# Sliding-window and linear attention in one kernel: value products as full matmuls, token sums in strips, a range check and a new order

## Chip, core and metric

One NeuronCore of one Trainium2 chip runs the whole program. The metric is device microseconds of one execution. Three runs of the kernel before gave 276.16, 276.88 and 277.05, median 276.88.

## What is computed

Two independent attention blocks, A and B, on inputs of 2048 tokens by 640 features (bf16), 32 heads of 20. A is softmax attention in which a token sees itself and the 255 before it; B is linear attention. Their outputs stand side by side in the result.

```python
# A
qkv = (x @ wqkv) split into q, k, v; heads of 20
scores = q k^T * 20**-0.5, kept where 0 <= i - j < 256
o = softmax(scores) v;  a = o @ wo
# B
phi(t) = where(t > 0, t + 1, exp(t)) + 1e-6
kv = phi(k)^T v;  z = sum over tokens of phi(k)
o = (phi(q) kv) / (phi(q) . z + 1e-6);  b = o @ wo
out = concatenate([a, b])
```

## The kernel before

**Order of the work.** Nothing is scheduled by a compiler. `build` describes some hundreds of operations to a `Planner` (line 56): each has the engines that may do it with an assumed duration, a key (its priority), the operations it depends on, and buffer slots. `Planner.run` (line 101) then plays the program through with these durations, takes the operation with the lowest key on each engine whenever the engine is free, and emits it at that point. So the instruction order of each engine is fixed when the program is built. On the chip every engine works its list in order and waits on semaphores. Nearly all DMAs are issued by one queue, SP, also in order; `dma` operations have keys and earliest times like the others.

**A.** Queries and keys of 512 tokens at a time (four tiles, t = 0 to 3) are projected by `proj` (line 374; matmuls at line 385) as 128x512 products. Heads are 20 wide and the tensor engine is addressed in strips of 32 rows, so 16 heads land in the tile `even` and the others are rearranged into `odd` by SBUF transfers on SP (lines 409 and 412). `proj_v` (line 426) makes the values: for each block of 64 tokens it issues two half-width matmuls per step (line 439), one for each half of the array's columns, so that a block's values of one set of heads come out on partitions 0 to 63 and those of the other set on 64 to 127. `attn` (line 463) then runs groups of heads: the score matmuls S (line 495) into the only big PSUM buffer, an exponential on ScalarE (line 507) with no maximum subtracted, masks on VectorE (line 517), and the product of probabilities and values, PV (line 538), with eight small tiles of the array side by side. Each value row carries a 21st column of ones, so PV gives the softmax sums too. The result goes to DRAM (`OD`, line 561) and comes back in another layout (`oc`, line 597; the sums alone as `osum`, line 601). Its reciprocal is taken by a logarithm and an exponential on ScalarE (lines 608 and 612), VectorE scales `oc` (line 621), and `finish_rows` (line 568, matmuls at line 573) multiplies by A's output matrix and stores.

**B.** `b_keys` (line 656) makes phi of the keys, `pk`. `b_sums` (line 673, matmuls at line 684) makes x^T phi(k); `b_z` (line 695) the token sums of phi(k), by 80 matmuls with one column of ones (line 714); `b_kvwo` (line 727) folds the value matrix and B's output matrix into one 640x640 matrix, which goes through DRAM for a new layout. `b_query` (line 802) makes phi of the queries (matmuls at line 811, evacuation at lines 636, 640 and 643), the denominator (`den`, line 823), its reciprocal (lines 827 and 834), scales (line 842) and ends in `finish_rows` again.

**The start.** Ten matmuls on a zeroed tile (line 855) run first. The first 512 tokens of x come as rows in four transfers (`x0n`, line 874) and are transposed on TensorE (line 902); all later ones come by transposing DMAs (`load_x`, line 353). The first halves of A's query and key weights (`wqn`, `wkn`) are issued by ScalarE's queue, the rest by SP (line 350), and are copied into the strip layout on VectorE (lines 891 and 895).

The values' half-width matmul, which a sentence hardly says:

```python
tok = bb * P + 64 * k0
rhs = wv[:, kt, :].rearrange("p (a i n) -> p a i n", a=2, i=2)[:, :, i, :]
nc.tensor.matmul(psum(g, k0, [P, 2, 160])[64 * i : 64 * i + 64, :, :], lhsT=xb["t"][:, kt, tok : tok + 64], rhs=rhs, ..., tile_position=(0, 64 * i))
```

## Time and profile before

| what | value |
|---|---|
| median of 3 runs | 276.88 us |
| the profiled execution's own time | not listed beside the profile |
| its span, first to last instruction | 273.2 us |
| TensorE busy | 255.1 us, 93% |
| ScalarE busy | 190.1 us, 70% |
| VectorE busy | 183.8 us, 67% |
| values, line 439 | 320 matmuls, 26.0 us busy |
| token sums, line 714 | 80 matmuls, 3.5 us busy |
| mean granted TensorE clock | 0.988 |

Busy times of matmuls are pipelined: the sum of the means is larger than the busy time, and the distance between starts in the timeline tells what one costs. PE is TensorE, PEld its weight loads, DVE VectorE, ACT ScalarE, POOL GpSimd; SPq is the instruction queue of the engine that issues the DMAs. In a row of groups the busy time is followed by the mean of one and by the idle time ahead of the group with what ended it. PEclk is the clock that TensorE was granted, in tenths of full speed.

### The profile page before, as it was taken

How to read it: one execution, taken by the hardware profiler on the slowest of the kernel's cores; microseconds unless marked ns; L12 is line 12 of the kernel's file. 1: busy time of each engine (PE TensorE's matmuls, PEld its weight loads, DVE VectorE, ACT ScalarE, POOL GpSimd, SP SyncE). 2: the span in 40 equal slices, each digit the busy share in tenths (PEclk: the TensorE clock that was granted, in tenths of full speed). 3: DMA queues.
4: the chain of work that ended last, by engine and by line, in shares of the span. 5: the costliest groups of instructions: out<-in, count | busy, mean ns of one | idle time of the engine just before them, and what ended most of it. 6: DMA issues, size and time to landing. Idle time of an engine off the chain costs nothing.

```text
span 273.2 us, 9860 instructions
## 1 busy us (share of the span) xinstructions
PE 255.1 (93%) x4312; PEld 148.0 (54%) x4312; DVE 183.8 (67%) x453; ACT 190.1 (70%) x187; POOL 6.8 (2%) x49
## 2 busy tenths in 40 slices
PE   7599998998998999989999999999989999999594
PEld 3245664545454556545556667457544665656273
DVE  1586776886776786678545444457896777788574
ACT  2066769779976888787868768378989869963410
POOL 8000000000000000001000000000000000000000
PEclk9999999999999999999999999599999999999999
DMA  7955535934448397556661104613999331302523
GB/s 204 313 106 68 171 91 119 148 95 67 104 121 148 85 261 225 120 153 96 191 198 37 44 0 129 154 49 91 203 193 231 90 113 56 108 24 89 163 81 111
DMA packets 51947, 34.50 MB, mean 126 GB/s; under 512 B 32066, under 2 KB 50754, under 8 KB 51906
## 3 DMA queue, kind: packets, MB, share of 16 engines
q1 hardware_dynamic: 50594, 33.08, 50.1%
q10 hardware_dynamic: 1312, 0.82, 1.1%
q8 instruction: 33, 0.54, 0.9%
q14 instruction: 8, 0.07, 0.1%
HBM read 13.80 MB, written 10.26 MB: 88 GB/s over the span
## 4 chain that ended last, share of the span: by engine, by line
PE 77%; DMA 7%; DVE 5%; SPq 4%; ACT 4%; issue 2%; ACTq 0%
PE F L573 16%; PE F L385 15%; PE F L684 9%; PE S L495 8%; PE F L439 8%; PE F L538 7%; PE F L661 6%; PE F L811 6%; SPq L361 3%; DMA wkn<-in_A_wqkv_dram 2%; ACT p L507 2%; DMA out_dram<-osb 2%; DMA osum<-OD 2%; PE F L823 1%; PE F L714 1%
## 5 line engine op out<-in xcount | busy, mean ns | idle before, releaser
L507 ACT ACTIVATE p<-S 128x2048 bf16<-128x2048 f32 x76 | 141.0, 1855 | 38.1 <-PE S L495 36.7
L517 DVE TENSOR_TENSOR p<-p,strip 128x256 bf16<-128x256 bf16 (+2 forms) x140 | 49.3, 381 | 21.0 <-ACT p L507 20.6
L636 ACT ACTIVATE e<-F 128x320 bf16<-128x320 f32 (+1 forms) x52 | 24.5, 500 | 9.1 <-PE F L811 7.7
L385 PE MATMUL F<-xT,wq 128*128 128x512 bf16 x100 | 25.3, 380 | 4.4 <-DMA xT<-in_A_x_dram 1.8
L385 PE MATMUL F<-xT,wk 128*128 128x512 bf16 x100 | 27.8, 406 | 0.0
L303 DVE CAST osb<-F 128x320 bf16<-128x320 f32 x45 | 21.9, 489 | 8.6 <-PE F L573 8.2
L303 DVE CAST even<-F 128x512 bf16<-128x512 f32 x29 | 20.0, 688 | 9.6 <-PE F L385 9.4
L439 PE MATMUL F<-wv,xT 128*64 128x320 bf16 x320 | 26.0, 302 | 0.4 <-issue 0.4
L661 PE MATMUL F<-wkB,xT 128*128 128x320 bf16 x160 | 25.6, 300 | 0.0
L573 PE MATMUL F<-kvwo,pq 128*128 128x320 bf16 x160 | 23.4, 299 | 2.0 <-DVE pq L842 2.0
L811 PE MATMUL F<-xT,wqB 128*128 128x512 bf16 x100 | 24.4, 381 | 0.9 <-DVE pq L643 0.9
L573 PE MATMUL F<-woA,oc 128*128 128x320 bf16 x160 | 24.7, 299 | 0.1
L684 PE MATMUL F<-pk,xtok 128*128 128x320 bf16 x160 | 24.5, 300 | 0.0
L538 PE MATMUL F<-p,v 64*32 64x320 bf16 (+4 forms) x1440 | 22.2, 256 | 0.6 <-DVE pk L643 0.5
L303 DVE CAST ost<-F 128x512 bf16<-128x512 f32 x22 | 14.6, 687 | 11.7 <-PE F L538 11.6
L303 DVE CAST v<-F 128x320 bf16<-128x320 f32 x28 | 13.8, 493 | 11.6 <-PE F L439 11.2
L573 PEld LDWEIGHTS <-pq 128*128 128x128 bf16 x160 | 15.2, 98 | 10.2 <-DVE pq L842 3.6
L439 PEld LDWEIGHTS <-xT 128*64 128x64 bf16 x320 | 16.5, 109 | 7.2 <-issue 3.8
L538 PEld LDWEIGHTS <-v 64*32 64x32 bf16 x1440 | 17.2, 92 | 5.3 <-issue 4.3
L661 PEld LDWEIGHTS <-xT 128*128 128x128 bf16 x160 | 14.6, 98 | 9.1 <-issue 2.6
L573 PEld LDWEIGHTS <-oc 128*128 128x128 bf16 x160 | 15.1, 98 | 7.2 <-issue 1.0
L684 PEld LDWEIGHTS <-xtok 128*128 128x128 bf16 x160 | 14.6, 98 | 7.8 <-issue 2.1
(71 smaller groups left out, 226.4 us busy)
## 6 DMA issues: line engine op xcount, KB each, us to landing
out_dram<-osb SPq DMA_DIRECT2D x32, 160.0 KB
OD<-ost SPq DMA_DIRECT2D x32, 128.0 KB
oc<-OD SPq DMA_DIRECT2D x4, 640.0 KB
xtok<-in_B_x_dram SPq DMA_DIRECT2D x4, 640.0 KB
odd<-even SPq DMA_DIRECT2D x32, 48.0 KB
odd<-st SPq DMA_DIRECT2D x32, 32.0 KB
wv<-in_A_wqkv_dram SPq DMA_DIRECT2D x1, 800.0 KB
wkB<-in_B_wqkv_dram SPq DMA_DIRECT2D x1, 800.0 KB
```

The lines of the kernel that those rows point to most:

```text
L303: nc.vector.tensor_copy(out=dst, in_=src)
L385: nc.tensor.matmul(ps[:], lhsT=w[:, kt, i, :], rhs=xb["t"][:, kt, :], start=(kt == 0), stop=(kt == KT - 1))
L439: nc.tensor.matmul(psum(g, k0, [P, 2, 160])[64 * i : 64 * i + 64, :, :], lhsT=xb["t"][:, kt, tok : tok + 64], rhs=rhs, start=(kt == 0), st ...
L495: nc.tensor.matmul(st["s"][64 * i : 64 * i + 64, j, c : c + b - a], lhsT=kb["t"][32 * j : 32 * j + Dh, sl, ko : ko + 64], rhs=qb["t"][32 * ...
L507: nc.scalar.activation(out=pb["t"][:, :, 0:n], in_=st["s"][:, :, 0:n], func=ACT.Exp, scale=scale)
L517: (nc.vector if e == "DVE" else nc.gpsimd).tensor_tensor(out=x, in0=x, in1=mkv[:, None, :].to_broadcast([P, 4, 64 * w]), op=ALU.mult)
L538: nc.tensor.matmul(O[i][32 * j : 32 * j + 32, a:b], lhsT=V[bl // 2]["t"][64 * i : 64 * i + 64, 336 * (bl % 2) + HV * n_ : 336 * (bl % 2) + ...
L573: return lambda ps: nc.tensor.matmul(ps[:], lhsT=lhs(c), rhs=rhs(c, hf), start=(c == 0), stop=(c == KT - 1))
L636: nc.scalar.activation(out=eb["t"][:, 0:n], in_=ps[:], func=ACT.Exp)
L661: return lambda ps: nc.tensor.matmul(ps[:], lhsT=xb["t"][:, kt, b * P : (b + 1) * P], rhs=R["wkB"][:, kt, hf * HALF : (hf + 1) * HALF], st ...
L684: return lambda ps: nc.tensor.matmul(ps[:], lhsT=R["xt", tb // 4][:, tb % 4, c * P : (c + 1) * P], rhs=R["pk", tb // 4][:, tb % 4, hf * HA ...
L811: return lambda ps: nc.tensor.matmul(ps[:], lhsT=R["wqB"][:, kt, :].rearrange("p (f c) -> p c f", c=KT)[:, c, :], rhs=xb["t"][:, kt, :], s ...
```

## The change

1. **Values.** `proj_v` multiplies 128 tokens by 320 columns at full width: 160 matmuls instead of 320. Each value tile now holds its tokens where they fall (64-token blocks on alternating partition halves). What PV needs on the other half is copied there by SBUF transfers on SP, two for each 256 tokens, 16 in all, into tiles `sw`; PV reads `vt` or `sw`. The ones columns are written once at the start instead of in each tile.
2. **Token sums.** 32 matmuls with 32 columns of ones as weights, each in one of four column strips of the array and 320 columns wide, give the sums of the four tiles in 32 equal rows each; two VectorE passes for each half split them into a high and a low bf16 part, and 10 one-column matmuls with 1/32 add and turn them.
3. **First loads.** ScalarE's queue issues only the first half of the query weights; the key half goes to SP behind x; the values' weights move back. The first two query groups are done in halves of 256 tokens. Weight copies may go to ScalarE. Five warm-up matmuls instead of ten.
4. **Range check.** For each tile of A two VectorE passes count how many softmax sums are at least 1e-18 and at most 1e18; after the last, a flag is made by one small matmul and two VectorE instructions. At the end every engine loads the flag and branches over a general path (`general`) that computes A again with a maximum subtracted. With these inputs the branch is taken and nothing of the path runs.
5. **Order.** The planner's durations, latencies and DMA model are new, and a table `TUNE` sets the key of nearly every operation and the earliest time of the DMAs. A's output groups of the last tile now stand between the last denominator and B's last output groups; `osum` is issued ahead of `oc`; the result of `b_sums` shares a buffer with `wqB`, which is loaded behind the kv products. Output buffers are 4 instead of 5, one feature buffer ring has 2 instead of 3.

The sums that the flag rests on (`chk`) stand in VectorE's list ahead of the last feature group of B, and the flag's matmul in TensorE's list after two of the last five denominator matmuls.

```diff
-PRM = {}
+PRM = {"pvw": 3412, "look": 78, "slack": 624}
+TUNE = {
+    "x0n0": -191500, "@x0n0": 0, "x0n1": -147458, ...
...
 def proj_v(t, key0, dkey):
-        for bb in range(4):
+        for hb in range(2):
             box = v_r.box()
...
-                            nc.tensor.matmul(psum(g, k0, [P, 2, 160])[64 * i : 64 * i + 64, :, :], lhsT=xb["t"][:, kt, tok : tok + 64], rhs=rhs, ..., tile_position=(0, 64 * i))
+                        return lambda ps: nc.tensor.matmul(ps[:], lhsT=xb["t"][:, kt, bb * P : bb * P + P], rhs=rhs_(), start=(kt == 0), stop=(kt == KT - 1))
...
+                    if i == 1:
+                        nc.sync.dma_start(out=sws[slot][64:128, :, :], in_=vts[slot][0:64, :, 336:684])
+                    else:
+                        nc.sync.dma_start(out=sws[slot][0:64, :, :], in_=vts[slot][64:128, :, 0:348])
...
 def em_pv
+                                if bl % 2 == i:
+                                    lhsT = vts[slot][64 * i : 64 * i + 64, vb, 336 * i + HV * n_ : 336 * i + HV * n_ + 32]
+                                else:
+                                    lhsT = sws[slot][64 * i : 64 * i + 64, vb, HV * n_ : HV * n_ + 32]
...
 def a_out(t, key0, dkey):
+        def chk(e, k):
+            nc.vector.tensor_scalar(out=OD[t]["junk"]["t"][:], in0=st["s"][:], scalar1=(LO, HI)[k], scalar2=0.0, op0=(ALU.is_ge, ALU.is_le)[k], op1=ALU.add, accum_out=R["cnt"][:, 2 * t + k : 2 * t + k + 1])
...
 def b_z(key):
-            return lambda ps: nc.tensor.matmul(ps[:, c : c + 1], lhsT=R["pk", tb // 4][:, tb % 4, :].rearrange("p (f c) -> p c f", c=KT)[:, c, :], rhs=ones[:], start=(tb == 0), stop=(tb == NT - 1))
+            for b in range(4):
+                for hf in range(2):
+                    for s in range(4):
+                        nc.tensor.matmul(ps[hf][32 * s : 32 * s + 32, :], lhsT=ones[:], rhs=R["pk", s][:, b, hf * HALF : (hf + 1) * HALF], start=(b == 0), stop=(b == 3), tile_position=(0, 32 * s), skip_group_check=True)
...
+            nc.vector.tensor_copy(out=hl["t"][:, 0, cs], in_=psum(zg, hf)[:])
+            nc.vector.tensor_tensor(out=hl["t"][:, 1, cs], in0=psum(zg, hf)[:], in1=hl["t"][:, 0, cs], op=ALU.subtract)
...
+            return lambda ps: nc.tensor.matmul(ps[:, c : c + 1], lhsT=hl["t"][:, w, :].rearrange("p (f c) -> p c f", c=KT)[:, c, :], rhs=c32[:], start=(w == 0), stop=(w == 1))
...
-    nwarm = PRM.get("nwarm", 10)
+    nwarm = PRM.get("nwarm", 5)
...
-    load_w("ACTQ", "wk0", lambda: wkn[:, :, 0:320], ...)
-    load_w("SP", "wv", lambda: wv[:], ...)
+    load_w("SP", "wk0", lambda: wkn[:, :, 0:320], ...)
...
+        nc.tensor.matmul(psum(fg, 0, [1, 2 * NTT])[:], lhsT=ones[:, 0:1], rhs=R["bad"][:], start=True, stop=True)
...
     pl.run(dry)
+    if not dry and not PRM.get("noguard"):
+        general(pools["tc"], nc, mk, R["flag"], xA, A_wqkv, A_wo, ident, out2, scale)
...
+def general(tc, nc, mk, flag, xA, A_wqkv, A_wo, ident, out2, scale):
+    v = nc.values_load(flag[0:1, 0:1], min_val=0, max_val=1024, ...)
+    with tc.If(v > 0):
...
```

749 lines of the change are left out of this document (475 added, 274 removed), and 53 rows, old and new, of tables (TUNE, left).

## Prediction

> **What bounds the kernel now.** I read the page first: engines, clock row, chain. TensorE is busy for 93% of the span and carries 77% of the chain that ended last; every other engine is at 70% or less. So the time is TensorE's own work plus the few places where it stands still or runs slowly.
>
> ```profile
> span 273.2 us, 9860 instructions
> PE 255.1 (93%) x4312; PEld 148.0 (54%) x4312; DVE 183.8 (67%) x453; ACT 190.1 (70%) x187; POOL 6.8 (2%) x49
> ...
> PEclk9999999999999999999999999599999999999999
> ...
> PE 77%; DMA 7%; DVE 5%; SPq 4%; ACT 4%; issue 2%; ACTq 0%
> ```
>
> The reader is to see one slow slice in the clock row. I then asked for busy time by stretch (us, PE, PEld, DVE, ACT, POOL, granted clock, DMA share, GB/s), to find the 18.1 us in which TensorE is idle and the stretch at half clock:
>
> ```profile
> 7.00:10.50 3.50, 0.80 (x7) 0.53 (x8) 1.99 (x6) 0.00 (x0) 0.00 (x0) 1.00 1.09 354
> ...
> 171.85:175.26 3.41, 3.41 (x38) 1.62 (x39) 1.00 (x3) 1.88 (x1) 0.00 (x0) 0.50 1.00 187
> 175.26:178.68 3.42, 3.42 (x54) 1.29 (x59) 1.72 (x3) 0.56 (x1) 0.00 (x0) 0.50 0.01 1
> ...
> 245.00:258.00 13.00, 10.57 (x98) 6.33 (x88) 8.04 (x18) 5.19 (x10) 0.00 (x0) 1.00 0.43 132
> 258.00:273.20 15.20, 11.04 (x80) 7.75 (x80) 9.62 (x21) 2.46 (x5) 0.00 (x0) 1.00 0.24 86
> ```
>
> Idle: 4.6 us up to 10.5, 2.4 in 245 to 258, 4.2 after 258, and the rest, 6.9, spread between. Last, the timeline and the chain, for what stands at those places:
>
> ```profile
> 1.25 3.97 PE L855 MATMUL F<-warm 128*128 128x512 bf16 x10 [1.25 <-DVE ones L326]
> ...
> 10.15 2.32 PE L385 MATMUL F<-xT,wq 128*128 128x512 bf16 x10 [1.64 <-DVE xT L303]
> ...
> 169.15 2.69 PE L714 MATMUL F<-ones,pk 128*128 128x1 bf16 x64
> ...
> 172.99 4.43 PE L385 MATMUL F<-xT,wk 128*128 128x512 bf16 x10
> ...
> 258.47 2.21 PE L573 MATMUL F<-kvwo,pq 128*128 128x320 bf16 x15 [2.03 <-DVE pq L842]
> ```
>
> Ten matmuls of one shape take 2.32 us at 10.15 and 4.43 us at 172.99, behind the token sums; the ten warm-up matmuls take 3.97, so the start runs at half clock too, though the clock column says 1.00 there.
>
> **Values (V).** 320 half-width matmuls go, 160 full ones come. The chain gives 1.48 us for 20 of the old ("18.55 1.48 PE F L439 x20") and 0.80 for 10 standing alone; five full ones of the new shape take 0.68 (L573 x5). That is 0.12 less for each of 16 blocks that stand together and up to 0.12 for each of 32 half blocks: 1.9 to 3.8. The busy column says less (26.0 us for L439 against 23.4 to 25.6 for 160 of L573, L661, L684): 0.4. I take **-2.4**, nearest to the chain, which has both kinds of block; ends -0.4 and -3.8.
>
> The 16 new transfers (half a value block to the other 64 partitions) cost SP 0.4 to 0.75 us each (rows OD<-ost 0.38, odd<-even 0.75 for one): 6 to 12 us of a queue that waits over 90 us in its own list of waits, so nothing by itself. But the product of probabilities and values now waits for cast, issue and landing instead of the cast: +3 us per block (0.49 cast, 0.4 to 0.75 issue, about 2 flight, as OD<-ost issued at 246.2 lands at 247.9). Cover: other groups in TensorE's order. Price without it: a rival.
>
> **Token sums.** 80 matmuls of one column (3.5 us busy; 2.52+0.73 in the chain) become 32 of 320 columns in four column strips and 10 of one column. If four strips run side by side the 32 are eight steps; the nearest row is PV, 12 steps in tiles of 64x32 in 1.35 us, so about 1.0 to 1.25. If they don't, 32 x 0.136 = 4.35. The 10 cost 3.5/80 each, 0.44. I take 1.7: **-1.8**, ends -2.1 and +1.3. The four DVE passes added (4 x 0.49) lie beside TensorE's other groups; only Zc, needed 35 us later, waits.
>
> The half clock behind them lasts from 171.85 to 178.68. Beside the 2.13 us lost in "173.13 4.29 PE F L385 x10" (10 x 0.216 otherwise), PV takes 1.70 instead of 1.35 and two S groups 0.4 more: **-2.9** if it goes. It is the only such stretch, and it directly follows the only long run of one-column matmuls, so I expect it to go; otherwise 0.
>
> **Start.** Before, TensorE begins at 10.15, because x's last 128 rows are waited for until 8.06 while the second weight half shares the DMA engines through ACT's queue. Now only x (640 KB) and wq's half (400 KB) come first: 0.35 MB by 3.5 us, then 312 GB/s (stretch 3.5 to 7), so 1.07 MB by 5.8. Transposes 0.45, casts 0.48 each; the first group works in halves of 256 columns and needs only the first two blocks, and ACT does wq's copy (about 0.6): start near 6.8, **3.3 earlier** if the clock is up. It may not be. The five warm-ups last 5 x 0.427 = 2.1 us. In this trace the clock rose at 4.6 after 3.35 us of matmuls from 1.25, and the stretch 171.85 to 175.26, with 2.3 us of wide matmuls in it, didn't raise it; the next one, full, did. Those edges lie on one grid of 3.41 us (4.60, 171.85, 175.26, 178.68), whose next points at the start are 8.01, 11.43, 14.84. Raised at 11.43, work from 6.8 runs 4.6 us at half rate: 2.3 of the 3.3 are lost; at 14.84, 4.0 are lost, and the start is 0.7 later than before. I take 11.43: **-1.0**, ends -3.3 and +0.7.
>
> The Trainium skill (TensorE: Matmul & The Clock Gate, Part 1) says that the array starts at half rate and is let up after a sustained busy window of about 3.4 us; that speaks against five warm-ups. The trace agrees on the 3.41 us. By that rule alone the sum for the start is the -1.0 or +0.7 above, never -3.3.
>
> **Tail.** Before: after the last PV (ends 245.53) TensorE waits 1.7 (254.34 to 256.07, last feature group's evacuation) and 2.0 (until 258.47, ln, exp, scaling). After: 30 output groups of A stand between the last den matmuls and B's last groups, so both waits have work beside them. New: the range check. Its two DVE passes stand in DVE's queue ahead of the last feature group and wait for the osum transfer, and one small TensorE matmul of the flag waits for them, ahead of den and A's groups. From PV's end, before's OD transfers land at +3.9 (249.4); issue 0.6 and about 2.5 flight put osum at +7; two passes (0.29 each) and the group's remainder (1.5) put the flag at +9.1, oc at about +9.5. TensorE gets there after 17 x 0.216 + 35 x 0.136 + 2 x 0.216 = 8.9. I count 1.0 of standing for 3.7: **-2.7**, ends -3.7 and 0. The other six checks (0.29 each) fall where DVE is at 67%.
>
> **End.** Every engine now loads the flag and branches over the general path. On SP it is behind the last store, whose landing (270.1 to 271.8) and close (273.2) leave 1.4 to 3 us of cover; loading and a jump over unfetched code have no row. Nearest: a wait between first instructions 0.3, an instruction packet 0.55, a small transfer 2. Ends 0 and +2.5; **+0.8**.
>
> **Order.** The 6.9 us of spread idle: 1.8 is waiting for A's transposed x (72, 115 and 116 us), whose issues stand earlier in SP's new order; 1.3 is ACT held by a logarithm for osum, now issued ahead of the larger oc. The rest is small waits that a new order can as well make as remove. One load gets later: wqB (800 KB) now takes the buffer of the sums' result and waits for the kv products; from the nearest row (wkn, 400 KB, 6.53 us in the chain at the start) it is 4 to 6.5 us until B's queries can begin, covered by the last A tile's groups, about 4 if that cover is gone. Smaller edits cost nothing beside this: output buffers 4 for 5, one feature buffer fewer, five wider kv products (under 0.1 us), q's halves (10 x 0.109 for 5 x 0.216). I take **-1.0**, ends -5 and +4, since V's longer way to PV pulls the other way.
>
> **Sum:** -2.4 -1.8 -2.9 -1.0 -2.7 +0.8 -1.0 = -11.0. The span goes to 262.2. The profiled execution's own time is not listed; its span stands 3.7 below the median of the runs, 276.88, and I leave this 3.7: **265.9**.
>
> **Rivals.**
> 1. Late swapped values (slower). SP issues in order; a swap behind transposed loads of 1.2 us each, or behind a wait for ost (up to 11.9 us in SP's waits), holds PV, and TensorE's queue is in order. Price 3 us for a swap with no cover. It decides from 11 us on: 0.7 us on each of 16 PV groups, or four groups without cover (4 x 3 = 12: 277.9). Then 277 to 280. For it: PE already waits at such places; against it: TensorE has 245 us of other work, and most swaps are listed well ahead of PV.
> 2. The clock is raised only at 14.84: +1.7, 267.6. For it: the row of 171.85, which was not raised either; against it: from 8 on there is wide work without a gap.
> 3. The strips don't run side by side: +3.1 on the sums, 269.0; or they leave the half clock in place: +2.9, 268.8. Against: PV's row shows tiles side by side.
> 4. The guard is exposed, load and fetch behind everything: +1.7, 267.6.
> 5. The new order also closes the spread idle: 5 instead of 1, 261.9.
>
> **How the numbers follow.** Forecast 0.46; rival 5 0.14; rivals 2, 3, 4 together 0.25; rival 1 0.15, of it 0.03 within 0.3%. A measurement of this kernel tells about 0.3% (0.8 us) from no change. The range takes in rivals 2 to 5 and most of the unknown ends: 260.5 to 273. Faster 0.85, same 0.03, slower 0.12.
>
> **What would show it.** V's line at some 23 to 25 us busy with 160 matmuls; the strips at 1.0 to 1.3 us with no 0.5 slice behind them; the first wq matmuls at about 7, 0.22 us each for 256 columns up to 11.4, then 0.11; no 2 us wait at the end of the tail; the last store followed by no more than 4 us. Wrong would be: waits of PE for a transfer of sw, a wait at the flag above 2 us, or a second stretch at half clock.

## The result and the profile after

The changed kernel took 279.56 us, the median of four runs (278.27 to 280.34), beside 276.86 for the kernel before on the same chip: a ratio of 1.0102, 95% interval [1.0053, 1.0151]. It is 1% slower. The forecast was 265.9, in a range of 260.5 to 273.0. Executions of one kernel spread by up to 4% here, and the ratios count only those within 1.5% of the kernel's fastest, so where few of them count I give the medians of all runs as well.

The profiled execution took 278.27, with a span of 276.6: 3.4 more than before. These are lines of the page of the changed kernel: span, TensorE's busy time, the clock row, and the shares of the chain that ended last.

```profile
span 276.6 us, 9513 instructions
...
PE 252.8 (91%) x4120; PEld 146.9 (53%) x4120; DVE 185.2 (67%) x469; ACT 193.6 (70%) x192; POOL 5.7 (2%) x29
...
PEclk9999999999999999999999999997999899999998
...
PE 66%; DMA 12%; SPq 10%; ACT 4%; DVE 3%; issue 3%; DVEq 0%
```

TensorE is busy 2.3 us less than before (255.1), as it should be, but it stands idle 23.8 us instead of 18.1. In the chain its share fell from 77% to 66%, and DMA and SP's queue grew from 11% to 22%. The slow slice of the clock row at 172 is gone, and two others have come. The trace's clock records give them exactly: half clock from 186.34 to 189.76 and from 213.65 to 217.06, 6.83 us together, as long as the one stretch before (171.85 to 178.68). At the start the clock is up only at 12.26 (before 4.60).

Four rows of TensorE's timeline of the changed kernel tell most of it (start, duration, the instructions, and in brackets the idle time ahead of them with what ended it):

```profile
8.36 3.60 PE L498 MATMUL F<-xT,wq 128*128 128x256 bf16 x16 [0.85 <-DVE wq L403]
...
174.31 1.27 PE L878 MATMUL F<-pk,ones 128*32 128x320 bf16 x32
...
185.39 0.33 PE L629 MATMUL S<-even 20*64 20x320 bf16 x4 [2.64 <-issue]
...
212.49 0.72 PE L717 MATMUL F<-kvwo,pq 128*128 128x320 bf16 x4 [2.30 <-DMA kvwo<-kvd]
```

The first query group starts 1.8 us earlier than before, but at half clock. The strips take 1.27 (forecast: about 1.0 to 1.25). Then come two stands that the kernel before does not have, one of 2.64 that waits for nothing but "issue", in the middle of a group, and one of 2.30 for the block matrix `kvwo`. Each half-clock window opens behind one of them.

To place the loss I summed, matmul by matmul, what each trace has put through TensorE (0.216 us for 512 columns, as in the rows) and compared when equal work was done. The changed kernel minus the kernel before:

| place (time before) | difference, us |
|---|---|
| first query groups done (12.2) | 0.0 |
| just ahead of the sums (169) | -0.8 |
| behind the sums (184) | -5.6 |
| B's block products made (194) | -0.3 |
| behind `kvwo` (221) | +3.0 |
| ahead of the tail (246) | +4.2 |
| last products (269) | +1.2 |
| end of the span | +3.4 |

So the sums and the tail gave what was forecast (4.8 and 3.0). The time came back in three places: right behind the sums, around `kvwo`, and at the end of the program.

Here is SP's queue in the changed kernel, with the loads that those stands hang on:

```profile
174.13 0.40 SPq L916 DMA_DIRECT2D wvB<-in_B_wqkv_dram  x1
174.63 0.55 SPq L923 DMA_DIRECT2D wo<-in_B_wo_dram  x1
...
182.43 0.38 SPq L981 DMA_DIRECT2D wqB<-in_B_wqkv_dram  x1
...
200.99 6.33 SPq L473 DMA_TRANSPOSE xT<-in_B_x_dram  x4
207.50 1.03 SPq L974 DMA_DIRECT2D kvwo<-kvd  x1
```

And the same loads in the kernel before, with the products that read the first of them:

```profile
167.25 0.39 SPq L730 DMA_DIRECT2D wvB<-in_B_wqkv_dram  x1
167.79 0.42 SPq L737 DMA_DIRECT2D wo<-in_B_wo_dram  x1
...
186.58 1.26 PE L747 MATMUL F<-GT,wvB 128*120 128x120 bf16 x20
```

Before, B's value weights (800 KB) are issued 19.3 us ahead of their first use; now it is 6.0 us (174.13 to 180.13), with 750 KB of B's output matrix right behind them and, new in this place, 800 KB of `wqB`. Before, `wqB` was issued at 125.84. Of the 13.3 us that the value weights have lost, 6.4 are an earlier use, and 6.9 a later issue: the new order lists them behind other transfers.

### The profile page after: what moved, and what is told of

The parts are those of the page before. It is cut to its first block, busy times and chain, and to the rows that moved or that the text cites. A ratio compares the mean times of both kernels' runs of the same rounds, so it can differ in the third digit from the quotient of the medians.

```text
span 276.6 us, 9513 instructions
## 1 busy us (share of the span) xinstructions
PE 252.8 (91%) x4120; PEld 146.9 (53%) x4120; DVE 185.2 (67%) x469; ACT 193.6 (70%) x192; POOL 5.7 (2%) x29
## 4 chain that ended last, share of the span: by engine, by line
PE 66%; DMA 12%; SPq 10%; ACT 4%; DVE 3%; issue 3%; DVEq 0%
PE F L717 14%; PE F L498 12%; PE F L842 8%; PE S L629 8%; PE F L560 6%; PE F L997 5%; PE F L817 5%; SPq L473 4%; PE F L683 4%; DMA xT<-in_A_x_dram 3%; ACT p L645 3%; DMA wvB<-in_B_wqkv_dram 2%; DMA kvwo<-kvd 2%; SPq L530 2%; DMA x0n<-in_A_x_dram 2%
## 5 line engine op out<-in xcount | busy, mean ns | idle before, releaser
L560 PE MATMUL F<-wv,xT 128*128 128x320 bf16 x160 | 27.6, 305 | 1.5 <-DVE st L403 1.1
L717 PE MATMUL F<-woA,oc 128*128 128x320 bf16 x160 | 26.7, 300 | 2.1 <-DMA odd<-even 2.1
L498 PE MATMUL F<-xT,wq 128*128 128x512 bf16 (+1 forms) x110 | 27.6, 382 | 1.0 <-DVE wq L403 0.9
L817 PE MATMUL F<-wkB,xT 128*128 128x320 bf16 x160 | 27.6, 300 | 0.0
L997 PE MATMUL F<-xT,wqB 128*128 128x512 bf16 x100 | 26.6, 392 | 0.2 <-DVE ost L403 0.2
L403 DVE CAST even<-F 128x512 bf16<-128x512 f32 x25 | 17.2, 688 | 12.9 <-PE F L498 12.7
L683 PE MATMUL F<-p,vt 64*32 64x320 bf16 (+3 forms) x720 | 21.6, 254 | 0.0
L683 PE MATMUL F<-p,sw 64*32 64x320 bf16 (+3 forms) x720 | 21.1, 254 | 0.0
L560 PEld LDWEIGHTS <-xT 128*128 128x128 bf16 x160 | 14.9, 99 | 9.8 <-issue 2.7
L817 PEld LDWEIGHTS <-xT 128*128 128x128 bf16 x160 | 15.0, 98 | 9.7 <-issue 2.1
L629 PE MATMUL S<-even 20*64 20x320 bf16 (+4 forms) x720 | 16.6, 264 | 3.6 <-issue 2.6
L683 PEld LDWEIGHTS <-vt 64*32 64x32 bf16 x720 | 16.5, 91 | 4.7 <-issue 4.1
```

What stands on the lines that cost most here:

```text
L403: nc.vector.tensor_copy(out=dst, in_=src)
L498: nc.tensor.matmul(ps[:, a:b], lhsT=w[:, kt, i, :], rhs=xb["t"][:, kt, a:b], start=(kt == 0), stop=(kt == KT - 1))
L560: return lambda ps: nc.tensor.matmul(ps[:], lhsT=xb["t"][:, kt, bb * P : bb * P + P], rhs=rhs_(), start=(kt == 0), stop=(kt == KT - 1))
L629: nc.tensor.matmul(st["s"][64 * i : 64 * i + 64, o0 : o0 + b - a], lhsT=kb["t"][32 * j : 32 * j + Dh, sl, ko : ko + 64], rhs=qb["t"][32 * ...
L683: nc.tensor.matmul(O[i][32 * j : 32 * j + 32, a:b], lhsT=lhsT, rhs=pb["t"][64 * i : 64 * i + 64, o0 : o0 + b - a], start=(cnt == 0), stop= ...
L717: return lambda ps: nc.tensor.matmul(ps[:], lhsT=lhs(c), rhs=rhs(c, hf), start=(c == 0), stop=(c == KT - 1))
```

## The experiments

The theory at the start: the change's terms are right where they stand, and the time comes back through transfers that are now late. The main rival: the cost lies in the added work itself (cold start, guard, swaps). Each run below was timed beside the kernel before, and its ratio is to that kernel. The changed kernel has four timed runs, all in the result above, so a difference from it is a difference of two ratios.

### The start alone

Ten warm-ups for five, no other edit.

```diff
-        for _ in range(nwarm):
+        for _ in range(10):
```

> The changed kernel with ten warm-up matmuls rather than five; nothing else differs, in order or in work. Theory (cold start): in the changed kernel the clock reached full at 12.26, against 4.60 before, so the work from 8.36 to 12.26 ran at half rate and lost about 1.9 us. With ten warm-ups it is up by 4.6 and the first weight matmuls, sixteen of 256 columns, take 1.7 to 1.9 us rather than 3.60; the span is 1.5 to 2 us shorter (time ratio to the kernel before about 1.003 rather than 1.010). Rival (given back): the earlier start only makes TensorE wait longer for the next loads on SP's queue (the wait at 40.0 grows from 0.8 to 2.5), and the time stays within 0.5 us of the changed kernel's.

Measured: ratio 1.0098 [1.0048, 1.0147], against 1.0102 without. The clock was up at 3.94, the sixteen matmuls took 1.92 instead of 3.60, and at the same VectorE instructions the kernel was 2.7 us ahead of the changed one at 19 to 38 us. Then the lead came and went. By 43 us 1.0 of it was gone, with waits of 0.50 and 0.82 for odd<-even at 37 and 38 where the changed kernel has one of 0.84; at 87 all of it was, behind a half-clock window that opened at 79.04; at 96 to 113 it was 2.1, and from 125 to the end 0.3 to 0.6. The rival holds in its result: what the start gains is given back. SP's queue took some of it by name; for the rest no single cause is shown.

### The guard at the end

The flag load, the branch and the general path left out.

```diff
-    if not dry and not PRM.get("noguard"):
+    if False:
```

> The changed kernel without the general path: the flag's load on every engine, the branch and the code of the exact path are left out; the range checks and the matmul of the flag still run. So inputs outside the checked range would not be handled. Theory (guard at the end): from the start of the last evacuation the changed kernel takes 5.9 us to its end, the kernel before 3.65; without load and branch the end is 2 to 2.3 us shorter and the time ratio to the kernel before falls from 1.010 to about 1.002. Rival (the end is set by the last store's landing and the closing of the program in any case): under 0.5 us.

Measured: 1.0043 [0.9984, 1.0102], so some 1.6 us off 1.0102, with intervals that overlap. The traces give more: from the start of the last evacuation to the end of the span it is 3.65 us before, 5.89 in the changed kernel and 3.2 in this run, so 2.7 for the guard. Nothing else is left of the difference of the two spans (273.9 against 276.6), although in this execution the clock was up at 4.59, and the kernel was 3.0 ahead at 20 to 39 us: a second case of a start whose gain was given back. The last pair of runs below prices the guard again.

### The load of kvwo

On SP's queue, `kvwo` behind one transposed load instead of four.

```diff
+        if self.held is not None and e == "SP" and o.name.startswith("ldy"):
+            self.seen += 1
+            if self.seen > HOLD:      # HOLD = 1
+                self.held.append(o)
+                return
         o.emit(e)
+        if o.name == "kvr":
+            for x in self.held:
+                x.emit("SP")
```

> The changed kernel with one move on SP's queue: the load of the block matrix kvwo stands behind one transposed load of B's x rather than behind four; the other three follow it. Theory (head of the queue): the wait of 2.30 us at 212.49 goes (kvwo is issued about 4.7 us earlier), and the half-clock window of 3.41 us that began at 213.65, 1.2 us behind that wait, goes with it, another 1.7 us: together 3 to 4 us, time ratio to the kernel before about 0.997 rather than 1.010. Rival A (the window is not caused by the wait): only 2.3 us, with a half-clock stretch still near 213. Rival B: TensorE waits for the three later transposed loads instead, and under 1 us is gained.

Measured: 0.9996 [0.9944, 1.0048], 2.9 us off the changed kernel. The wait fell from 2.30 to 1.02 and no half-clock window opened near 213. One place in SP's order cost 1%.

```profile
210.52 0.72 PE L734 MATMUL F<-kvwo,pq 128*128 128x320 bf16 x4 [1.02 <-DMA kvwo<-kvd]
```

### Fewer bytes behind the sums

B's output matrix filled with zeros by GpSimd instead of loaded.

```diff
-            nc.sync.dma_start(out=R["wo6"][:], in_=B_wo[0:600, :]...)
-            nc.sync.dma_start(out=R["wo6b"][:], in_=B_wo[520:640, :])
+            nc.gpsimd.memset(R["wo6"][:], 0.0)
+            nc.gpsimd.memset(R["wo6b"][:], 0.0)
```

> The changed kernel without the load of B's output matrix: its two tiles are filled with zeros by GpSimd instead of two transfers of 800 KB in all that stood at 174.6 to 175.3 (so B's output is wrong in values; the matmuls and all else still run). Theory (TensorE's instruction fetch behind bulk transfers): TensorE stood 2.64 us at 182.75 with no dependency, while its next 16 KB of instructions were fetched only at 182.87; with 800 KB less on the DMA engines in that stretch the fetch comes in time, the stand goes, and so does the half-clock window at 186.34 behind it (1.7 us more): 3.5 to 4.3 us, time ratio to the kernel before about 0.995. Rival A: the stand stays, since it is the loads of x and wvB, not these, that hold the fetch, or since it has another cause; under 0.5 us gained. Rival B: the stand goes, the half-clock window stays: 2.6 us.

Measured: 0.9869 [0.9783, 0.9954], more than expected (the two loads are 900 KB, not 800). The stand at 183 and its window were gone. The list of DMA packets suggests why the stand was there: TensorE's instructions come in 33 packets of 16 KB, one for each 250 or so. In the changed kernel one came at 172.73 and the next only at 182.87, behind the bulk loads; without these 900 KB it came at 177.80.

### The same bytes later

The two loads three issues later on SP.

```diff
+        if o.name == "ld.wo6":
+            self.late = [o, LATE]      # LATE = 3, counted in SP's operations
+            return
```

> The changed kernel with one move on SP's queue: the two loads of B's output matrix stand three issues later (behind a store and two transfers of ost), near 181 rather than 174.6 us; all the work is done. Theory (TensorE's instruction fetch waits behind bulk transfers): the 16 KB of instructions that came at 182.87 are fetched at about 177.8, as in the run without these loads, and the stand of 2.6 to 2.9 us near 183 goes, with the half-clock window behind it where there was one (1.7): 2.6 to 4.3 us, time ratio to the kernel before 0.995 to 1.000. Rival A (the run without the loads gained because less was moved at all): the stand stays or comes back at the first product that reads these loads (near 188), and less than 1 us is gained. Rival B (the loads of x and the first weight matrix hold the fetch): stand unchanged.

Measured: 1.0105 [1.0063, 1.0146]: nothing gained. The instructions came in time (180.26) and TensorE ran on, into the data, as rival A had it for this run. A row of the timeline of an execution of 282.18, among the slowest of the twelve (the next run, of 275.19, shows the same wait):

```profile
188.57 0.79 PE L966 MATMUL F<-wo,kvT 120*120 120x320 bf16 x2 [4.47 <-DMA wo<-in_B_wo_dram]
```

So the fetch was only the first thing to be late. What is short is, by these two runs, the transfers' time between the sums and B's matrices.

### Four corrections together

`kvwo` earlier, the two loads later, ten warm-ups, no guard: the four edits above in one kernel.

> The changed kernel with four corrections together: the two loads of B's output matrix three issues later, kvwo's load behind one transposed load rather than four, ten warm-ups rather than five, and no flag load, branch or general path at the end (so that inputs outside the checked range would not be handled; the checks still run). If the causes are separate: about 3 (fetch) + 3 (kvwo) + 1.7 (guard) + 0 to 1 (warm-ups): 270 to 271 us, time ratio to the kernel before 0.975 to 0.985, close to the 265.9 forecast less what the sums, the values and the order gave too little. Rival (the gains overlap, since each shifts the stream into the other waits and other half-clock windows open): ratio 0.99 or more.

Measured: 0.9970 [0.9924, 1.0015]. The gains did not add up. TensorE waited 4.42 for `wo` again, and half clock lasted from 187.28 to 197.52.

### The values alone, and the sums alone, in the kernel before

```diff
-                        for i in range(2):
-                            ... lhsT=xb["t"][:, kt, tok : tok + 64], ..., tile_position=(0, 64 * i))
+                        nc.tensor.matmul(psum(g, k0, [P, 2, 160])[:], lhsT=xb["t"][:, kt, bb * P : bb * P + P], rhs=rhs, ...)
```

> The kernel before with one change: each block of A's values is made by five matmuls of all 128 columns of tokens rather than ten of 64 for each half; the casts go straight into the old tile, nothing is swapped between partitions (so A's values lie at wrong places and A's output is wrong in values; counts and sizes of all other work are the same). It prices the values' matmuls alone. By the forecast's term: 2.4 us shorter (ratio 0.991). By the busy columns of the two profiles (27.6 us for 160 against 26.0 for 320): nothing gained, or up to 1.6 us lost (ratio 1.000 to 1.006).

Measured: 1.0027 [0.9989, 1.0066]. In place the term is right: between the first start of each run of value matmuls and the next other matmul, waits left out, I count 24.57 us before and 22.37 with full products, 2.2 less (forecast 2.4). At the end of the kernel nothing of it can be seen. In its profiled execution half clock from 8.97 to 15.79 and from 258.14 to 261.55, where the kernel before has none, took more than that. In between it came from 3.3 behind at 50 us to 0.95 ahead at 221, and 1.7 of that can be the half clock behind the sums, which lasted one window there instead of two.

```diff
-        g = group([(0.04, mm(c, tb)) for c in range(KT) for tb in range(NT)], ...
+        zo = pl.op({"PE": 1.12}, emz, key, [pk_ops, list(g_mm)], mode="z", slots=(2, "F"), g=zg, name="z", cls="V")
+        ...      # emz: 32 matmuls in four strips; two DVE passes a half; 10 one-column matmuls
```

> The kernel before with one change: the token sums in four column strips (32 matmuls of 320 columns, four DVE passes, ten matmuls of one column) in place of eighty of one column. By the forecast's terms: 1.8 us for the sums and 2.9 for the half clock behind them, 4.7 in all, ratio 0.983, and no half-clock window at 172 to 179. Rival A (the half clock there has another cause than the one-column matmuls): 1.8 us, ratio 0.9935, the window stays. Rival B (what is gained is waited for again further on, as in the changed kernel): under 1 us.

Measured: 1.0117 [1.0071, 1.0164], by the medians of all runs 1.0058 (277.62 and 276.01). Nothing is gained. Two rows of its timeline:

```profile
173.80 1.27 PE L722 MATMUL F<-pk,ones 128*32 128x320 bf16 x32
...
201.59 0.38 PE L497 MATMUL S<-even 20*64 20x128 bf16 x17 [1.94 <-issue]
```

The sums are as fast as promised, no half-clock window follows them, and at equal work the kernel goes from 2.0 behind to 2.6 ahead across them: 4.6, the forecast's 4.7. Then it stands for instructions again, behind bulk loads (`wvB` was issued at 187.52 and read at 192.75), and half clock lasts from 202.71 to 209.53. But this run is not the strips alone: the planner, given other durations, made a new order behind the sums and issued `wvB` and the output matrix some 20 us later than the kernel before (167.25), and 2.0 of what it lost stood there at 19 us, long before the sums. So it shows the 4.6 in place, and that they do not reach the end in this order; what the strips are worth in the kernel before stays open.

### B's matrices early

The buffers of A's query and key weights are free from 138 us on. `wvB` and `wo` go there, issued at 151.6 and 144.1.

```diff
-            R["wvB"] = mk("over", [P, KT, D], BF16, "wvB", tag="T0")
+            R["wvB"] = mk("w", [P, KT, D], BF16, "wvB", tag="wq")
-            R["wo6"] = mk("over", [120, 5, D], BF16, "wo6", tag="T1")
+            R["wo6"] = mk("w", [120, 5, D], BF16, "wo6", tag="wk")
...
+        if o.name == "ow2":            # second issue of this name: wo6
+        if o.name == "osum1":          # then wvB
```

> The changed kernel with one move: the two loads of 800 and 750 KB that TensorE needs right behind the sums (B's value weights and most of B's output matrix) go into the buffers of A's query and key weights, which are free from 138 us on, and are issued near 142 and 150 rather than at 174; all the work is done, the other engines' order is the same. Theory (the sums' gain brings TensorE to B's matrices before they are there: the stand of 2.64 for instructions behind these transfers, or of 4.47 for the transfer itself when it was issued later, are two faces of it): no stand above 0.6 us between 176 and 192, no half-clock window there; 3 to 5 us shorter than the changed kernel, ratio to the kernel before 0.992 to 1.000. Rival A (the stand is of the instruction stream and has nothing to do with these transfers): it stays near 183. Rival B (moved traffic holds up odd<-even or x at 142 to 152, and the gain is lost there): a new wait of more than 1 us between 140 and 170.

Measured: 0.9859 [0.9823, 0.9895], 2.4% below the changed kernel, and the first version with all of the work that is faster than the kernel before. (Between the two profiled executions it is 3.7 us, 4.6 of them gained between 178 and 193 us.) Two stretches, busy time of the engines, granted clock, DMA share and GB/s; first the changed kernel:

```profile
180.00:184.00 4.00, 2.61 (x60) 2.33 (x60) 3.26 (x8) 1.66 (x1) 0.00 (x0) 1.00 1.04 270
184.00:188.00 4.00, 2.61 (x16) 1.70 (x17) 1.39 (x4) 1.88 (x1) 0.00 (x0) 0.79 0.86 274
```

and with the early loads:

```profile
180.00:184.00 4.00, 4.00 (x133) 3.38 (x124) 3.63 (x8) 2.42 (x3) 0.00 (x0) 1.00 0.44 152
184.00:188.00 4.00, 3.56 (x35) 2.04 (x33) 4.00 (x12) 3.93 (x4) 0.00 (x0) 1.00 0.93 296
```

The reader is to see that TensorE is busy 7.56 of 8 us instead of 5.22, at full clock, while the DMA engines move less in the first stretch. The order on the other engines is the same.

With `kvwo` earlier and no guard as well:

> The run before this one, with kvwo's load behind one transposed load rather than four, and without the flag load, branch and general path at the end (inputs outside the checked range would not be handled). If the three causes add up: 3 to 5 (early loads) + 3 (kvwo) + 1.7 (guard) off the changed kernel's 1.010, so a ratio of 0.975 to 0.985, the fastest of all. Rival (the stream, once faster, meets the next late transfer, as it did in the run with four corrections): 0.990 or more, with a wait above 2 us named in the trace.

Measured: 0.9716 [0.9659, 0.9773], median 268.95. Now the gains add up.

### The swaps

The sixteen swap transfers left out, then issued from another queue.

```diff
-                        nc.sync.dma_start(out=sws[slot][64:128, :, :], ...)      # and its twin
+                        pass
```

> The changed kernel without the sixteen transfers that swap half value blocks to the other partitions (their tiles hold ones from the start, so A's attention output is wrong in values; the order on every other engine is the same). Theory: no wait of TensorE in the changed kernel names these tiles, so their direct price is nothing, and what SP's queue is spared (about 10 us of issuing) shortens only the small waits for odd<-even and x at 40, 67 and 91: 0 to 1.5 us, ratio 1.005 to 1.010. Rival 1 of the forecast (swapped values hold the products of probabilities and values): 5 us or more, ratio below 0.992.

Measured: 0.9863 [0.9814, 0.9913], median 272.65. My theory falls: it gave 0 to 1.5 us. At equal work the kernel is 6.6 us ahead of the changed one at 133 us, although both had the clock up only at about 12.5. The time lies in small waits: TensorE stands 2.1 us instead of 7.7 in the stretches 20 to 40, 60 to 100 and 120 to 130 together. None of those waits names a swapped tile. They name odd<-even, x, and casts, whose transfers stand behind the swaps. SP's queue in the changed kernel:

```profile
25.31 0.71 SPq L576 DMA_DIRECT2D sw<-vt  x1
26.12 0.61 SPq L574 DMA_DIRECT2D sw<-vt  x1
26.82 4.01 SPq L530 DMA_DIRECT2D odd<-even  x5
30.95 0.68 SPq L576 DMA_DIRECT2D sw<-vt  x1
31.72 0.65 SPq L574 DMA_DIRECT2D sw<-vt  x1
32.43 2.95 SPq L533 DMA_DIRECT2D odd<-st  x4
35.42 2.31 SPq L530 DMA_DIRECT2D odd<-even  x3
```

and without the swaps:

```profile
26.60 3.96 SPq L531 DMA_DIRECT2D odd<-even  x5
30.67 2.87 SPq L534 DMA_DIRECT2D odd<-st  x4
33.58 2.31 SPq L531 DMA_DIRECT2D odd<-even  x3
```

Over these ten us the queue has no gap above 0.2 us. The four swaps take 2.65 us of it, the last odd<-even begin 1.8 us later (35.42 against 33.58), and for those TensorE waits at 40.01. Fifteen of the sixteen swaps are issued without a wait of their own; one, at 193.48, has stood 6.7 us at the head of SP's queue for its cast, and all behind it with it.

```diff
-                        nc.sync.dma_start(out=sws[slot][64:128, :, :], ...)
+                        nc.gpsimd.dma_start(out=sws[slot][64:128, :, :], ...)
```

> The changed kernel with its sixteen swap transfers issued from GpSimd's queue rather than SP's; the order on the other engines is the same and all the work is done. Without these transfers the kernel was 2.4% faster (6.6 us gained by 133 us). Theory A (SP's queue: each swap takes 0.7 us of issuing and holds what stands behind it while it waits for the casts): most of it comes back, ratio to the kernel before 0.985 to 0.997, and the waits for odd<-even at 40 and x at 67 and 69 shrink. Theory B (the swapped values come late, or the traffic of 1.4 MB is the price): it stays within 2 us of the changed kernel, ratio 1.003 or more, with waits of TensorE at products of p.

Measured: a median of 274.03 (six runs, 269.13 to 276.32) beside 276.36 before, a ratio of 0.992 and inside theory A's range; no interval can be given. The waits at 40 and at 69 are gone and the one at 67 is 0.47. The trace is 5.5 us shorter than the changed kernel's; 2.8 of its lead stood there at 20 us, since the clock was up at 5.35.

> The fastest version so far (early loads of B's matrices, kvwo's load behind one transposed load, no general path at the end, so that inputs outside the checked range would not be handled) with the swap transfers on GpSimd's queue. If what the swaps cost is SP's queue, 2 to 5 us off its 0.972: ratio 0.955 to 0.965. If not: 0.970 to 0.975.

Measured: 0.9476 [0.9410, 0.9542], median 262.46, faster than expected: 2.4% off the version with the swaps on SP, with the same work and bytes. So late values and the mere traffic are not the price; having the swaps on SP's queue is. The packets changed too. Of the DMA queues' packets, MB and share of the engines' time, first with the swaps on SP, then on GpSimd:

```profile
q1 hardware_dynamic: 53654, 35.02, 54.4%
...
q1 hardware_dynamic: 51350, 33.59, 54.7%
q0 software_dynamic: 768, 1.43, 2.7%
```

The swaps are 2304 packets of SP's queue in one case, 768 of another queue in the other. How much of the gain is the issuing time and how much the packets, no run separates; the rows of 25 to 38 us above show the issuing time at work. The Trainium skill (DMA: Bandwidth & Descriptors, Issuing engines are not separate DMA queues) says that starting transfers from several engines saves only the time on the sequencer to start them, usually small beside the transfer. One issue is small here too, 0.6 to 0.7 us beside a median of 3.8 from issue to landing on GpSimd's queue; sixteen of them, some 10 us of a queue that others wait for, came with 6.5 us of the kernel.

### The sums undone, and the kernel before with early weights

The eighty one-column matmuls put back into the changed kernel, as one planned group:

```diff
-        zo = pl.op({"PE": 1120}, emz, kv("z", key), [pk_ops, gm], mode="z", slots=(2, "F"), ...)
+        g = group([(42, mm(c, tb)) for c in range(KT) for tb in range(NT)], ..., kv("z", key), deps=[pk_ops, gm], chunk=16, name="z")
```

> The changed kernel with the token sums as before, eighty matmuls of one column and no strips; the rest is as changed, its order moves slightly behind the sums. By the forecast's terms it is 4.7 us slower than the changed kernel (1.8 for the sums, 2.9 for half clock behind them): ratio 1.027. By the theory that the strips' gain is given back at the transfers of B's matrices: the sums and a half-clock window cost their time again near 175, but the stand of 2.64 near 183 and its window go, so that the time stays within 1.5 us of the changed kernel's: ratio 1.004 to 1.015.

Measured: 1.0458 [1.0403, 1.0513], far above both expectations. Up to 200 us its trace keeps up with the changed kernel (about 2 us ahead at 198): the stand of 2.64 and its window are gone, as the theory has it. But the planner had another duration to plan with and made another order behind the sums; TensorE stands 4.3 us for ScalarE between 214 and 221 and 5 us more later on. This run tells nothing about the whole.

```diff
-            ps = [psum(zg, hf, [P, HALF]) for hf in range(2)] ...      # strips: emit nothing
+            pass
...
+                for tb in range(8 * w, 8 * w + 8):      # where each one-column matmul stood: eight
+                    nc.tensor.matmul(ps[:, c : c + 1], lhsT=R["pk", tb // 4]..., rhs=ones[:, 0:1], ...)
```

> The changed kernel with eighty matmuls of one column for the token sums, standing where its ten of one column stand; the strips and the DVE passes between are left out, and the order of every instruction around them on every engine and queue is that of the changed kernel, so that the order moves nothing as it did in the run before. Forecast's terms: 4.7 us slower than the changed kernel, ratio 1.027. Theory (the sums' gain is given back at B's matrices): the sums cost 1.8 more, a half-clock window may open behind them, the stand of 2.64 near 183 is gone or smaller; the time stays within 1.5 us of the changed kernel's, ratio 1.004 to 1.016.

Measured: 1.0227 [1.0155, 1.0300]; by the medians of all runs (280.20 and 277.30) it is 1.0105, like the changed kernel's. The profiled span is 276.4 against 276.6: the sums take 3.5 us instead of 1.8, the stand is 1.56 instead of 2.64, and half clock lasts from 183.26 to 190.09. At 195 us it is 1.9 behind the changed kernel; from 220 on it is level, since its wait for `kvwo` is 1.81 instead of 2.30 and no half-clock window follows. So trace and medians say that the strips' gain is given back in the changed kernel. But by the ratios they are worth 3.5 us, and the interval reaches from 1.5 to 5.5, which takes in the forecast's 4.7: these runs don't settle it.

And the eighth run's kernel with one load moved, behind the second transfer of ost that follows `osum1`:

```diff
-            R["wvB"] = mk("over", [P, KT, D], BF16, "wvB", tag="T0")
+            R["wvB"] = mk("w", [P, KT, D], BF16, "wvB", tag="wq")
...
```

> The kernel before with the token sums in strips, as in the eighth run, and one of B's loads (the value weights, 800 KB) put into the buffer of A's query weights and issued near 142 rather than 187.5 us. Theory (the sums gave 4.7 us in place, and the crowded transfers behind them took these back: 0.5 for the value weights, 1.9 for instructions at 201.6, and the half-clock stretch of 6.8 that followed): the waits at 192.8 and 201.6 and the stretch go, and the ratio comes to 0.983 to 0.992. Rival (the transposed loads of x, not the weights, crowd the queue at 192 to 204): the stand at 201.6 stays, ratio 1.005 to 1.012.

Measured: 0.9786 [0.9720, 0.9852]; by the medians of all runs (274.84 and 276.35) it is only 0.9946. Either way it is better than the eighth run (1.0117, and 1.0058 by medians), whose order it has but for this load. The wait at 192.8 is gone and the one for instructions is 0.68 instead of 1.94, while a half-clock stretch of 6.83 at 201.61 stayed: the theory holds in part.

### The last pair: the start again, and the guard

Ten warm-ups in the fastest version, then the same with the guard put back.

> The fastest version (early loads, kvwo's load earlier, swaps on GpSimd's queue, no general path, so that inputs outside the checked range would not be handled) with ten warm-ups rather than five. In its profile the clock rose only at 13.74. Theory: ten warm-ups raise it by 6.4 in every execution, and with SP's queue no longer full at 30 to 40 us what is gained at the start stays: 1.5 to 3 us, ratio 0.938 to 0.944 (0.9476 without). Rival (as in the changed kernel, the gain is waited for again): 0.945 to 0.950.

Measured: 0.9527 [0.9466, 0.9588]; medians 260.98 and 277.30 (0.941). The ratio is not below the 0.9476 of the version with five, and the intervals overlap. Beside that version's median of 262.46 the start is worth about 1.5 us, and at equal work the trace is ahead of that version's by 2.2 us at 19 us and by 3.0 at the end. So the theory is favoured, not shown.

> The run before with the flag load, branch and general path put back, so that it does all that the changed kernel does. The guard's price is the difference: by the profiles 2.0 to 2.3 us (forecast 0.8, ends 0 and 2.5), ratio about 0.008 above the run before: 0.946 to 0.953. It is the version that should beat both kernels with all of the work done.

Measured: 0.9630 [0.9564, 0.9696], medians 263.95 and 277.30. This version does all that the changed kernel does and beats both. The guard is the difference of the two, 3.0 us by the medians, 2.7 by the traces (from the last evacuation to the end 6.3 against 3.6). Its page:

```profile
span 261.0 us, 9496 instructions
...
PE 244.3 (94%) x4091; PEld 145.0 (56%) x4125; DVE 184.5 (71%) x469; ACT 193.5 (74%) x192; POOL 15.3 (6%) x45
...
PEclk9999999999999999999999999999999999999998
```

TensorE is idle 16.7 us instead of 23.8 (at most: 34 wide matmuls are missing from the records of this trace), and no half-clock window is left between 6.71 and the end of the work.

## Why the prediction was wrong

It added up TensorE's terms and took for granted that the transfers keep pace. Of its signs of being wrong one came, a second stretch at half clock; no wait named a swapped tile or stood at the flag. Term by term:

- **Values, -2.4.** Right in place: 2.2 in the kernel before (24.57 to 22.37), 1.0 in the changed kernel, where two blocks run at half clock. (The sign that it named, a busy time of 23 to 25, failed: it is 27.6, where the half-width ones had 26.0.) The step that failed is the next one: "6 to 12 us of a queue that waits over 90 us in its own list of waits, so nothing by itself". The sum of a queue's waits says nothing about the stretches in which it has none. Leaving the sixteen swaps out gave 6.6 us back, and moving them to another queue 6.5 in the fastest version. With them the term was worth +4 to +6, not -2.4.
- **Rival 1** was the slower case and had the right place, SP's in-order queue, and about the right end (277 to 280). Its mechanism was wrong: no product of probabilities and values waited for a swapped tile. It was the neighbours of the swaps that came late. So that its figure fits is luck.
- **Token sums and half clock, -1.8 and -2.9.** Right in place, 4.8 and 4.6 in two kernels, and given back within 20 to 30 us in both. The working asked what hides an added cost, and never what a saved one had been hiding. Before, B's value weights had 19.3 us between issue and use, and the slow sums lay in them. But the saving is only about half of what these weights lost; the later issue in the new order is the other half, and in the eighth run the order moved too. That the gain is given back when nothing else moves rests on one run, by its trace and medians (1.0105 against 1.0098).
- **Order, -1.0, ends -5 and +4.** Two misses of opposite sign. Up to the sums rival 5 was right: the rows of before have 5.3 us of waits (0.35 us and more each) between 46 and 138, those of the changed kernel without swaps only 1.7. The swaps filled the place with others. Behind the sums is the largest miss of all. The rows that would have warned of it were at hand (167.25 and 186.58, above): the working says that `wqB` gets later, and looked only at B's queries. It didn't set the loads behind the sums beside the time to their first use: 2.5 MB issued from 174.13 to 182.43, at the 270 to 284 GB/s that the stretch shows, are some 9 us of all DMA engines, and the first of them is read 6 us after its issue. Early loads alone were worth 2.4% (6.7 us), the place of `kvwo` 1% (2.9 us); by the spans of the traces it is 3.7 and 4.1.
- **Start, -1.0.** The clock was up at 12.26, between the 11.43 and the 14.84 weighed, and the gain in place was nothing. That it fits so well is partly luck: the grid of the other trace was used, and each execution has its own. Of the twelve profiles with five warm-ups eight have the clock up at 10.98 to 13.74, and four at 4.59 to 5.35, behind a window of which 2.9 to 3.2 us of 3.41 were busy. So the end of -3.3 does happen: the run without the guard, one of the four, was 3.0 ahead of the changed kernel at 20 us. What an early clock gains (2.7 us with ten warm-ups) is given back on the way in the changed kernel; in the fastest version 1.5 (medians) to 3.0 (traces) stayed, though the ratios don't show it.
- **Tail, -2.7.** Right: 3.0, and no wait at the flag.
- **End, +0.8.** Mis-sized: 2.2 against the kernel before, 2.7 against the same kernel without the guard, 2.7 to 3.0 in the last pair. The flag's load is 0.5 to 0.7 on each engine, and SP's list of waits has 2.5 behind the branch, which was costed as covered by the last store.

The sum as it came, by equal work: 0 at the start; -0.8 up to the sums (values -1.0, swaps +6.6, and the new order about -6, which is the remainder and was not tested); sums -4.8; behind them +5.3; around `kvwo` +3.3 and up to the tail 1.2 more; tail -3.0; end +2.2. That is 3.4 of span. With the transfers moved, ten warm-ups and all the work kept the kernel takes 263.95. That this lies near 265.9 doesn't confirm the sum: those moves are no part of the change, and but for one load the kernel before was not given them. The 3.7 between span and time, too, was 1.7 in the changed kernel.

## What to carry to other kernels

Before a saving on the busiest engine is booked, list the transfers whose issue-to-use distance runs across it, and subtract: a load that had 19 us and now has 6, by an earlier use and a later issue, can take the saving back. Read a DMA queue as a timeline around each added issue, not as a total of its waits; a cheap transfer in a stretch without gaps delays everything behind it, and the waits then carry other tiles' names. And price a stand of TensorE at nearly twice its length when it is long enough to drop the clock.

## What the runs showed of the hardware

- **The clock drops after one window that is only partly idle.** All edges of the clock records lie on a grid of 3.41 us that starts anywhere with respect to the kernel. Over the 20 profiles, between 20 and 255 us, every full-clock window in which TensorE stood 2.0 us or more (19 of them) was followed by a window at half clock; of those with 1.4 to 2.0 us, 14 of 25; of those with less, five: one with 1.39, and four right behind or within one-column matmuls. Ten of the profiles lack some records of matmuls, so that a stand can be shorter than it looks; in the ten that have all, the counts are 8 of 8 and 7 of 11. The same stand of 2.8 us lay across two windows in the run with `kvwo` earlier (183 to 186) and cost no window there. The Trainium skill (TensorE: Matmul & The Clock Gate, Part 1) has the free-running window of 3413 ns, which agrees, and puts the drop after at least one idle window; here 60% of one was enough, and such a stand of 2.0 us costs up to 1.7 us more (half of 3.41).
- **TensorE can run out of instructions.** The stands on "issue" of 2.64, 2.87, 2.81, 2.82, 2.79 and 2.39 us in six kernels all stood where a 16 KB packet of its instructions came behind 1.7 MB of bulk loads (in each the packet began within 0.5 us after the stand did), and went when those loads were moved or left out. Twice it was shorter: 1.56 with the old sums in place, 1.94 behind other loads (strips in the kernel before). That the packet waits for these loads and not for something beside them is what the moved loads show; how the two share the engines was not measured.
- **A flag's load and a branch at the end are not free.** They took 2.7 to 3.0 us beside the same kernel without them, with no instruction of the guarded path run.
